# Attention kernel: keys transposed in rows of eight, first load and last store in pieces, plain copies as 32-bit words

## The chip, the cores and the metric

One core of a Trainium2 chip. The metric is the device time of one execution in microseconds (us). The kernel before takes 1265.33 us, the median of three runs (1265.04 to 1265.5).

## The reference

Softmax attention over 16 x 32 = 512 heads, bf16 in and out: 192 queries, 1024 keys, head size 128.

```python
B, H, Sq, Sk, D = 16, 32, 192, 1024, 128      # q, k, v: normal * 0.05, bf16
scale = q.shape[-1] ** -0.5
scores = jnp.einsum("bhqd,bhkd->bhqk", q, k) * scale
p = softmax(scores, axis=-1)
return jnp.einsum("bhqk,bhkd->bhqd", p, v)
```

## The kernel before

**Units.** The 512 heads come in 32 groups of 16 (G). A group is eight pairs of heads, and a pair is three units of 128 query rows: rows 0 to 127 of head a, the same of head b, and the last 64 rows of a and b together (two matmuls side by side on column halves of the array, `tile_position`). So there are 768 units, 24 to a group; three units are called a triple here.

**A unit's way.** `qk` (L199): two matmuls of 512 keys each, queries stationary, keys `kt` moving, into a score tile `s_ps` (two buffers). `rowmax` (L296, VectorE): one pass that scales, copies the scores to `ss` and takes the row's extreme into `nb`. Then x = scores minus extreme: for units 0 and 1 of a triple GpSimd subtracts (`shift`, L184) and the exp comes later; for unit 2 ScalarE does the exp at once (`exp_first`, L349 on, instruction L356). `tr` (L236): eight 128x128 transposes of x by TensorE into `pt_ps`; each loads a block of x as the weights and multiplies by `ident`. `evac` (L362, ScalarE): from `pt_ps` to `pt_sb`, with the exp for units 0 and 1 (L367) and as a plain copy for unit 2 (L369). `pv` (L247): eight products of `pt_sb` blocks with `vs`, each with a product by `ones` for the row sum (L270) where ScalarE has not summed already. `onorm` (L313, VectorE): division, into `ob`.

**Which keys stand in which block.** `vs` holds key 8p+t on partition p in block t, because its load reads eight keys of a row group as one contiguous run. `kt` holds the keys in their order, so block t of the transposes is every eighth column of x (`X[:, t: SK: KT_TILES]`, L244).

**Order.** Each engine has its own program, tied by semaphores. TensorE's is written out by hand (L286 to L292): at step s it issues `qk(s+1)`, `tr(s-4)`, `pv(s-7)`.

**Transfers.** SP alone issues them, all on one queue, in this order for each group g: `loads(g+2)` = the transposing DMA of 16 heads of k (L141, 4 MB, after the last `qk` of group g), that of q (L144), the plain load of v (L149, after the last `pv` of g); then `stores(g)` = three DMAs (L158, L163, L164, after the last `onorm` of g). `kt`, `qt`, `vs` and `ob` have two buffers. At the start the loads of groups 0 and 1 are issued without a wait. `qk` of a group's first unit waits for that group's k and q (L203, L204), `pv` of it for v (L251).

Of the kernel before, what the change touches and what calls it, by code (L numbers as in the profile page):

```python
# [5 lines left out]
BF16 = mybir.dt.bfloat16  # L6
F32 = mybir.dt.float32
# [5 lines left out]
R_W = 2  # L13


def _attention_kernel(nc, q, k, v, out, G=16, NS=2, LAGS=(2, 4, 5, 7), ROUTES=(R_W, R_W, R_EA)):
    B, H, SQ, D = q.shape
    SK = k.shape[2]
    assert D == 128 and SK == 1024 and SQ == 192, (D, SK, SQ)
# [43 lines left out]
    with ExitStack() as es:  # L63
# [6 lines left out]
        def sem(name):  # L70
            return es.enter_context(nc.semaphore(name))

        kt = sb("kt", [128, NS, G * SK], BF16)
        qt = sb("qt", [128, NS, G * SQ], BF16)
        vs = sb("vs", [128, NS, G, KT_TILES, 128], BF16)
        ob = sb("ob", [128, NSO, PPG, 4, 128], BF16)
# [5 lines left out]
        rinv = sb("rinv", [128, 2, 4], F32)  # L82
        ones = sb("ones", [128, 128], BF16)
        ident = sb("ident", [128, 128], BF16)
        s_ps = [ps("s_ps%d" % i, [128, SK], F32) for i in range(2)]
        pt_ps = [ps("pt_ps%d" % i, [128, KT_TILES, 128], BF16) for i in range(2)]
        o_ps = [ps("o_ps%d" % i, [128, 4, 128], F32) for i in range(2)]
        s_setup = sem("s_setup")
        sxk = [sem("sxk%d" % i) for i in range(NS)]
        sxq = [sem("sxq%d" % i) for i in range(NS)]  # L90
        svl = [sem("svl%d" % i) for i in range(NS)]
        sst = [sem("sst%d" % i) for i in range(NSO)]
        s_qk = sem("s_qk")
        s_max = sem("s_max")
# [17 lines left out]

        O_SLOT = (0, 2, 1)

        def load_cnt(g):
            return 16 * (g // NS + 1)

        def store_cnt(g):
            return 48 * (g // NSO + 1)
# [12 lines left out]

        @block.sync
        def _(e):
            def loads(g):
                s = g % NS
                last_u = (g - NS + 1) * UPG - 1
                h0 = g * G
                if g >= NS:
                    e.wait_ge(s_qk, last_u + 1)  # L140
                e.dma_start_transpose(  # L141
                    kt[:, s], kf[h0:h0 + G].rearrange("g k d -> (g k) d")
                ).then_inc(sxk[s], 16)
                e.dma_start_transpose(  # L144
                    qt[:, s], qf[h0:h0 + G].rearrange("g k d -> (g k) d")
                ).then_inc(sxq[s], 16)
                if g >= NS:
                    e.wait_ge(s_pv, last_u + 1)
                e.dma_start(  # L149
                    vs[:, s], vf[h0:h0 + G].rearrange("g (p t) d -> p g t d", t=KT_TILES)  # L150
                ).then_inc(svl[s], 16)

            def stores(g):
                so = g % NSO
                e.wait_ge(s_on, (g + 1) * PPG)
                h0 = g * G
                og = of[h0:h0 + G]
                e.dma_start(  # L158
                    og[:, 0:128, :].rearrange("h p d -> p h d"),
                    ob[:, so].rearrange("p pg (x y) d -> p (pg x) (y d)", y=2)[:, :, 0:128],  # L160
                ).then_inc(sst[so], 16)
                oab = og[:, 128:192, :].rearrange("(pg x) p d -> x p pg d", x=2)
                e.dma_start(oab[0], ob[0:64, so, :, 1, :]).then_inc(sst[so], 16)  # L163
                e.dma_start(oab[1], ob[64:128, so, :, 1, :]).then_inc(sst[so], 16)  # L164

            for g in range(min(NS, NGR)):
                loads(g)
            for g in range(NGR):
                if g + NS < NGR:
                    loads(g + NS)  # L170
                stores(g)
            for so in range(min(NSO, NGR)):
                n_uses = len(range(so, NGR, NSO))
                e.wait_ge(sst[so], 48 * n_uses)

        @block.gpsimd
# [21 lines left out]
        def _(pe):  # L198
            def qk(u):  # L199
                pr, k3, g, pg = unit_info(u)  # L200
                s = g % NS
                if u % UPG == 0:
                    pe.wait_ge(sxk[s], load_cnt(g))  # L203
                    pe.wait_ge(sxq[s], load_cnt(g))  # L204
                if u >= 2:
                    pe.wait_ge(s_max, u - 1)
                S = s_ps[u % 2]
                a = 2 * pg
                b = 2 * pg + 1
                ins = None  # L210
                for c in range(2):
                    cs = slice(512 * c, 512 * c + 512)
                    if k3 < 2:
                        x = a if k3 == 0 else b
                        ins = pe.matmul(  # L215
                            S[:, cs],
                            qt[:, s, x * SQ: x * SQ + 128],
                            kt[:, s, x * SK + 512 * c: x * SK + 512 * c + 512],
                            start=True, stop=True,
                        )  # L220
                    else:
                        pe.matmul(  # L222
                            S[0:64, cs],
                            qt[:, s, a * SQ + 128: a * SQ + 192],
                            kt[:, s, a * SK + 512 * c: a * SK + 512 * c + 512],
                            start=True, stop=True, tile_position=(0, 0),
                        )
                        ins = pe.matmul(  # L228
                            S[64:128, cs],
                            qt[:, s, b * SQ + 128: b * SQ + 192],  # L230
                            kt[:, s, b * SK + 512 * c: b * SK + 512 * c + 512],
                            start=True, stop=True, tile_position=(0, 64),
                        )
                ins.then_inc(s_qk, 1)

            def tr(u):  # L236
                wait_x(pe, u)
                if u >= 2:
                    wait_evac(pe, u - 2)
                X = x_sb[:, u % NX, :]  # L240
                PT = pt_ps[u % 2]
                ins = None
                for t in range(KT_TILES):
                    ins = pe.transpose(PT[:, t, :], X[:, t: SK: KT_TILES], ident[:])  # L244
                ins.then_inc(s_tr, 1)

            def pv(u):  # L247
                pr, k3, g, pg = unit_info(u)
                s = g % NS
                if u % UPG == 0:  # L250
                    pe.wait_ge(svl[s], load_cnt(g))  # L251
                wait_evac(pe, u)
                if k3 == 0 and pr >= 2:
                    pe.wait_ge(s_on, pr - 1)
                O = o_ps[pr % 2]
                PTS = pt_sb[:, u % NPT]
                sl = O_SLOT[k3]
                a = 2 * pg
                b = 2 * pg + 1
                ins = None  # L260
                with_rs = route(u) == R_W
                for t in range(KT_TILES):
                    first = t == 0
                    last = t == KT_TILES - 1
                    if k3 < 2:
                        x = a if k3 == 0 else b
                        ins = pe.matmul(O[:, sl, :], PTS[:, t, :], vs[:, s, x, t, :],  # L267
                                        start=first, stop=last, skip_group_check=True)
                        if with_rs:
                            ins = pe.matmul(O[:, 3, sl: sl + 1], PTS[:, t, :], ones[:, 0:1],  # L270
                                            start=False, stop=last, skip_group_check=True)
                    else:
                        pe.matmul(O[0:64, sl, :], PTS[:, t, 0:64], vs[:, s, a, t, :],  # L273
                                  start=first, stop=last, skip_group_check=True, tile_position=(0, 0))
                        ins = pe.matmul(O[64:128, sl, :], PTS[:, t, 64:128], vs[:, s, b, t, :],  # L275
                                        start=first, stop=last, skip_group_check=True, tile_position=(0, 64))
                        if with_rs:
                            pe.matmul(O[0:64, 3, sl: sl + 1], PTS[:, t, 0:64], ones[:, 0:1],
                                      start=False, stop=last, skip_group_check=True, tile_position=(0, 0))
                            ins = pe.matmul(O[64:128, 3, sl: sl + 1], PTS[:, t, 64:128], ones[:, 0:1],  # L280
                                            start=False, stop=last, skip_group_check=True, tile_position=(0, 64))
                ins.then_inc(s_pv, 1)
# [12 lines left out]
        def _(dve):  # L295
            def rowmax(u):  # L296
                dve.wait_ge(s_qk, u + 1)
                if u >= NSS:
                    wait_x(dve, u - NSS)
                dve.tensor_scalar(  # L300
                    ss[:, u % NSS, :], s_ps[u % 2][:], -scale, None, ALU.mult, ALU.min,
                    accum_out=nb[:, u % NSS: u % NSS + 1],
                ).then_inc(s_max, 1)

# [43 lines left out]
        def _(act):  # L348
# [13 lines left out]
            def evac(u):  # L362
# [3 lines left out]
                if route(u) == R_W:  # L366
                    act.activation(pt_sb[:, u % NPT], pt_ps[u % 2][:], ACT_FN.Exp, scale=-1.0).then_inc(s_eva, 1)  # L367
                else:
                    act.activation(pt_sb[:, u % NPT], pt_ps[u % 2][:], ACT_FN.Copy).then_inc(s_eva, 1)  # L369

            for step in range(NU + L_EV + 1):
                u = step - L_EV
# [43 lines left out]
```

## Time and profile before

| | us |
|---|---|
| median of three runs | 1265.33 |
| span of the profiled execution, first to last instruction | 1263.1 |
| so around the span | 2.2 |
| TensorE busy (matmuls / weight loads) | 1234.2 / 1009.4 |
| VectorE / ScalarE / GpSimd busy | 1102.0 / 1048.6 / 960.4 |
| bytes moved | 321.89 MB, 255 GB/s over the span |
| first matmul / first `pv` | 21.0 / 33.2 |
| last `pv` matmul issued / last instruction | 1256.6 / 1263.1 |

A group line of the profile reads: source line, engine, operation, output <- inputs, shapes, count, then total busy time and the mean ns of one; behind the bar the idle time of the engine just before. PE is TensorE's matmul side and PEld its weight loads. In the timeline and the chain of waits the first column is the start and the second the duration, both in us. SPq is SyncE's queue: the duration of a DMA there is the time in which it is issued, not that in which it lands.

### The profile page before, as it was taken

The page shows a single profiled execution, that of the slowest core. Times are in us where ns is not written, and L with a number is a line of the kernel's source. Part 1 is how long each engine was busy: PE and PEld are TensorE (multiplying, and loading weights), DVE is VectorE, ACT ScalarE, POOL GpSimd, SP SyncE. Part 2 cuts the span into 40 slices and gives each one's busy share as a digit, 9 for nine tenths or more (in the row PEclk, how much of TensorE's full clock was granted, in tenths as well). Part 3 has the DMA queues.
Part 4 walks back from the last instruction along what each step waited for, and adds up shares of the span by engine and source line. Part 5 has one row for each costly group of instructions (what it writes and reads, how often), then busy time and mean ns, then how long its engine had stood idle before and what let it go on. Part 6 is the DMA issues. An engine that isn't in the chain of part 4 may idle for free.

```text
span 1263.1 us, 48658 instructions
## 1 busy us (share of the span) xinstructions
PE 1234.2 (98%) x20480; PEld 1009.4 (80%) x20480; DVE 1102.0 (87%) x2304; ACT 1048.6 (83%) x1281; POOL 960.4 (76%) x518
## 2 busy tenths in 40 slices
PE   3999999999999999999999999999999999999997
PEld 1888888888888888888888888888888888888886
DVE  2889888898988989898898988889898898989885
ACT  1888888888888888888888888888888888888886
POOL 2778777777877778787777877777787777878774
PEclk9999999999999999999999999999999999999999
DMA  9999999999999999999999999999999999999941
GB/s 288 268 261 240 278 280 266 288 270 245 254 269 261 279 233 255 281 275 262 261 230 272 271 276 268 252 251 272 272 267 281 253 263 252 271 261 281 244 118 27
DMA packets 790743, 321.89 MB, mean 255 GB/s; under 512 B 724992, under 2 KB 724992, under 8 KB 790528
## 3 DMA queue, kind: packets, MB, share of 16 engines
q1 hardware_dynamic: 790528, 318.78, 108.8%
q8 instruction: 164, 2.69, 0.8%
q14 instruction: 51, 0.42, 0.1%
HBM read 134.22 MB, written 25.17 MB: 126 GB/s over the span
## 4 chain that ended last, share of the span: by engine, by line
PE 97%; SPq 1%; DMA 1%; ACT 0%; issue 0%; DVE 0%; ACTq 0%
PE pt_ps L244 33%; PE o_ps L267 24%; PE s_ps L215 18%; PE o_ps L273 11%; PE s_ps L222 9%; SPq L141 1%; DMA vs<-in_v_dram 1%; PE o_ps L270 1%; PE o_ps L275 1%; SPq L144 0%; PE s_ps L228 0%; ACT x_sb L356 0%; ACT pt_sb L367 0%; DVE ob L330 0%; DVE rinv L327 0%
## 5 line engine op out<-in xcount | busy, mean ns | idle before, releaser
L188 POOL TENSOR_TENSOR x_sb<-ss,nb 128x1024 bf16<-128x1024 f32 x512 | 959.7, 1895 | 288.9 <-PE pt_ps L244 266.8
L300 DVE TENSOR_SCALAR_CACHE_REDUCE ss<-s_ps 128x1024 f32<-128x1024 f32 x768 | 938.5, 1222 | 140.5 <-PE s_ps L215 110.8
L244 PEld LDWEIGHTS pt_ps<-ident,x_sb 128*128 128x128 bf16 x6144 | 487.1, 148 | 203.3 <-issue 105.4
L367 ACT ACTIVATE pt_sb<-pt_ps 128x1024 bf16<-128x1024 bf16 x512 | 521.0, 1018 | 41.9 <-PE pt_ps L244 41.8
L244 PE MATMUL pt_ps<-ident,x_sb 128*128 128x128 bf16 x6144 | 520.7, 228 | 0.2 <-ACT pt_sb L367 0.2
L267 PE MATMUL o_ps<-vs,pt_sb 128*128 128x128 bf16 x4096 | 403.0, 217 | 0.3 <-DMA vs<-in_v_dram 0.3
L369 ACT ACTIVATE pt_sb<-pt_ps 128x1024 bf16<-128x1024 bf16 x256 | 262.1, 1024 | 140.1 <-PE pt_ps L244 140.0
L270 PE MATMUL o_ps<-ones,pt_sb 128*128 128x1 bf16 x4096 | 376.0, 165 | 0.0
L267 PEld LDWEIGHTS o_ps<-vs,pt_sb 128*128 128x128 bf16 x4096 | 352.3, 97 | 0.5 <-DMA vs<-in_v_dram 0.4
L270 PEld LDWEIGHTS o_ps<-ones,pt_sb 128*128 128x128 bf16 x4096 | 340.7, 96 | 0.0
L215 PE MATMUL s_ps<-kt,qt 128*128 128x512 bf16 x1024 | 305.3, 379 | 21.3 <-DMA qt<-in_q_dram 21.0
L356 ACT ACTIVATE x_sb<-ss,nb 128x1024 bf16<-128x1024 f32 x256 | 292.3, 1142 | 23.6 <-DVE ss L300 23.6
L273 PE MATMUL o_ps<-vs,pt_sb 128*64 128x128 bf16 x2048 | 162.3, 222 | 0.0
L275 PE MATMUL o_ps<-vs,pt_sb 128*64 128x128 bf16 x2048 | 162.3, 222 | 0.0
L222 PE MATMUL s_ps<-kt,qt 128*64 128x512 bf16 x512 | 153.2, 381 | 0.6 <-DVE ss L300 0.5
L228 PE MATMUL s_ps<-kt,qt 128*64 128x512 bf16 x512 | 153.2, 381 | 0.0
L330 DVE TENSOR_TENSOR ob<-o_ps,rinv 128x384 bf16<-128x384 f32 x256 | 142.7, 557 | 8.7
L273 PEld LDWEIGHTS o_ps<-vs,pt_sb 128*64 128x64 bf16 x2048 | 121.0, 109 | 17.1
L275 PEld LDWEIGHTS o_ps<-vs,pt_sb 128*64 128x64 bf16 x2048 | 121.0, 109 | 0.0
L215 PEld LDWEIGHTS s_ps<-kt,qt 128*128 128x128 bf16 x1024 | 63.3, 96 | 23.6 <-issue 21.5
L300 DVE DVE_READ_ACCUMULATOR ss<-s_ps 128x1 f32 x768 | 64.0, 83 | 0.0
L356 ACT ACTIVATION_READ_ACCUMULATOR x_sb<-ss,nb 128x1 f32 x256 | 48.9, 191 | 0.0
(11 smaller groups left out, 165.7 us busy)
## 6 DMA issues: line engine op xcount, KB each, us to landing
vs<-in_v_dram SPq DMA_DIRECT2D x32, 4096.0 KB, 15.2
out_dram<-ob SPq DMA_DIRECT2D x32, 512.0 KB, 15.9
out_dram<-ob SPq DMA_DIRECT2D x64, 128.0 KB, 4.9
kt<-in_k_dram SPq DMA_TRANSPOSE x32, 21.4
qt<-in_q_dram SPq DMA_TRANSPOSE x32, 6.6
```

The source lines that it names most:

```text
L188: gp.tensor_tensor(x_sb[:, u % NX, :], ss[:, u % NSS, :], nb[:, u % NSS: u % NSS + 1].to_broadcast([128, SK]), ALU.subtract,).then_inc(s_x ...
L215: ins = pe.matmul(S[:, cs], qt[:, s, x * SQ: x * SQ + 128], kt[:, s, x * SK + 512 * c: x * SK + 512 * c + 512], start=True, stop=True,)
L222: pe.matmul(S[0:64, cs], qt[:, s, a * SQ + 128: a * SQ + 192], kt[:, s, a * SK + 512 * c: a * SK + 512 * c + 512], start=True, stop=True, ...
L244: ins = pe.transpose(PT[:, t, :], X[:, t: SK: KT_TILES], ident[:])
L267: ins = pe.matmul(O[:, sl, :], PTS[:, t, :], vs[:, s, x, t, :], start=first, stop=last, skip_group_check=True)
L270: ins = pe.matmul(O[:, 3, sl: sl + 1], PTS[:, t, :], ones[:, 0:1], start=False, stop=last, skip_group_check=True)
L273: pe.matmul(O[0:64, sl, :], PTS[:, t, 0:64], vs[:, s, a, t, :], start=first, stop=last, skip_group_check=True, tile_position=(0, 0))
L275: ins = pe.matmul(O[64:128, sl, :], PTS[:, t, 64:128], vs[:, s, b, t, :], start=first, stop=last, skip_group_check=True, tile_position=(0, ...
L300: dve.tensor_scalar(ss[:, u % NSS, :], s_ps[u % 2][:], -scale, None, ALU.mult, ALU.min, accum_out=nb[:, u % NSS: u % NSS + 1],).then_inc(s ...
L356: act.activation(x_sb[:, u % NX, :], ss[:, u % NSS, :], ACT_FN.Exp, bias=nb[:, u % NSS: u % NSS + 1], scale=-1.0, accum_out=rs[:, pr % NRS ...
L367: act.activation(pt_sb[:, u % NPT], pt_ps[u % 2][:], ACT_FN.Exp, scale=-1.0).then_inc(s_eva, 1)
L369: act.activation(pt_sb[:, u % NPT], pt_ps[u % 2][:], ACT_FN.Copy).then_inc(s_eva, 1)
```

## The change

1. **k** is read as rows of eight keys: a group's k is seen as 2048 rows of 1024 elements, and the transposing DMA writes `kt` as [128, 8, 2048]: block t holds key 8p+t of every head. A `qk` matmul now reads four runs of 128 columns, 4 KB apart, in place of one run of 512; the scores come out in the order of blocks, so that the transposes take packed runs of 128 columns.
2. **First group** loaded in three pieces (heads 0-1, 2-7, 8-15), each with semaphores of its own, in the order k0 q0, k1 q1 v0 v1, k2 q2 v2. **Last group** stored in four pieces (pairs 0-3, 4-5, 6, 7), three DMAs each.
3. **Plain copies** of unit 2 (L369) treat two bf16 numbers as one 32-bit word.

```diff
-def _attention_kernel(..., ROUTES=(R_W, R_W, R_EA)):
+def _attention_kernel(..., ROUTES=(R_W, R_W, R_EA),
+                      FIRST=((0, 2), (2, 8), (8, 16)), LAST=((0, 4), (4, 6), (6, 7), (7, 8))):
...
-        kt = sb("kt", [128, NS, G * SK], BF16)
+        kt = sb("kt", [128, NS, KT_TILES, G * 128], BF16)
...
+        def words(t):
+            return t.rearrange("p t q -> p (t q)").bitcast(F32)
...
+            def load_kq(g, a, b, sems):
+                s = g % NS
+                h0 = g * G
+                e.dma_start_transpose(
+                    kt[:, s, :, a * 128:b * 128],
+                    kf[h0 + a:h0 + b].rearrange("g (p t) d -> (g p) (t d)", t=KT_TILES),
+                ).then_inc(sems[0], 16)
+                e.dma_start_transpose(
+                    qt[:, s, a * SQ:b * SQ],
+                    qf[h0 + a:h0 + b].rearrange("g r d -> (g r) d"),
+                ).then_inc(sems[1], 16)
...
-            for g in range(min(NS, NGR)):
+            n = len(FIRST)
+            for i in range(n):
+                load_kq(0, *FIRST[i], (sf[i], sf[i]))
+                if i > 0:
+                    for i2 in range(i if i > 1 else 0, i + 1):
+                        load_v(0, *FIRST[i2], sfv[i2])
+            for g in range(1, min(NS, NGR)):
                 loads(g)
             for g in range(NGR):
                 if g + NS < NGR:
                     loads(g + NS)
-                stores(g)
+                for a, b in (LAST if g == NGR - 1 else ((0, PPG),)):
+                    stores(g, a, b)
...
-                if u % UPG == 0:
+                if g == 0:
+                    for i, (h, _) in enumerate(FIRST):
+                        if u == 3 * h // 2:
+                            pe.wait_ge(sf[i], 32)
+                elif u % UPG == 0:
                     pe.wait_ge(sxk[s], load_cnt(g))
                     pe.wait_ge(sxq[s], load_cnt(g))
...
-                    ins = pe.transpose(PT[:, t, :], X[:, t: SK: KT_TILES], ident[:])
+                    ins = pe.transpose(PT[:, t, :], X[:, t * 128:t * 128 + 128], ident[:])
...
-                    act.activation(pt_sb[:, u % NPT], pt_ps[u % 2][:], ACT_FN.Copy).then_inc(s_eva, 1)
+                    act.activation(words(pt_sb[:, u % NPT]), words(pt_ps[u % 2][:]), ACT_FN.Copy).then_inc(s_eva, 1)
```

Not shown: the same split of `loads` and `stores` into pieces a to b, `pv`'s waits for the pieces of v (`sfv`), and the counts of the semaphores.

More of the change, by code (lines that the diff above doesn't have):

```diff
@@ L13, with _attention_kernel @@
 R_W = 2
-def _attention_kernel(nc, q, k, v, out, G=16, NS=2, LAGS=(2, 4, 5, 7), ROUTES=(R_W, R_W, R_EA)):
+def _attention_kernel(nc, q, k, v, out, G=16, NS=2, LAGS=(2, 4, 5, 7), ROUTES=(R_W, R_W, R_EA),
+                      FIRST=((0, 2), (2, 8), (8, 16)), LAST=((0, 4), (4, 6), (6, 7), (7, 8))):
     B, H, SQ, D = q.shape
@@ L84, in _attention_kernel @@
         ident = sb("ident", [128, 128], BF16)
-        s_ps = [ps("s_ps%d" % i, [128, SK], F32) for i in range(2)]
+        s_ps = [ps("s_ps%d" % i, [128, KT_TILES, 128], F32) for i in range(2)]
         pt_ps = [ps("pt_ps%d" % i, [128, KT_TILES, 128], BF16) for i in range(2)]
@@ L91, in _attention_kernel @@
         svl = [sem("svl%d" % i) for i in range(NS)]
+        sf = [sem("sf%d" % i) for i in range(len(FIRST))]
+        sfv = [sem("sfv%d" % i) for i in range(len(FIRST))]
         sst = [sem("sst%d" % i) for i in range(NSO)]
@@ L113, in _attention_kernel @@
         O_SLOT = (0, 2, 1)
+        def words(t):
+            return t.rearrange("p t q -> p (t q)").bitcast(F32)
         def load_cnt(g):
-            return 16 * (g // NS + 1)
+            return 16 * (g // NS + 1 - (g % NS == 0))
         def store_cnt(g):
@@ L134, in _, with load_v @@
         def _(e):
+            def load_kq(g, a, b, sems):
[9 more added lines that the diff above has]
+                ).then_inc(sems[1], 16)
+            def load_v(g, a, b, sm):
+                h0 = g * G
+                e.dma_start(
+                    vs[:, g % NS, a:b],
+                    vf[h0 + a:h0 + b].rearrange("g (p t) d -> p g t d", t=KT_TILES),
+                ).then_inc(sm, 16)
             def loads(g):
@@ L137, in loads, with stores @@
                 last_u = (g - NS + 1) * UPG - 1
-                h0 = g * G
                 if g >= NS:
                     e.wait_ge(s_qk, last_u + 1)
[L141 to L146, printed above, removed]
+                load_kq(g, 0, G, (sxk[s], sxq[s]))
                 if g >= NS:
                     e.wait_ge(s_pv, last_u + 1)
[L149 to L153, printed above, removed]
+                load_v(g, 0, G, svl[s])
+            def stores(g, a, b):
                 so = g % NSO
-                e.wait_ge(s_on, (g + 1) * PPG)
-                h0 = g * G
-                og = of[h0:h0 + G]
+                e.wait_ge(s_on, g * PPG + b)
+                og = of[g * G + 2 * a:g * G + 2 * b]
                 e.dma_start(
                     og[:, 0:128, :].rearrange("h p d -> p h d"),
-                    ob[:, so].rearrange("p pg (x y) d -> p (pg x) (y d)", y=2)[:, :, 0:128],
+                    ob[:, so, a:b].rearrange("p pg (x y) d -> p (pg x) (y d)", y=2)[:, :, 0:128],
                 ).then_inc(sst[so], 16)
                 oab = og[:, 128:192, :].rearrange("(pg x) p d -> x p pg d", x=2)
-                e.dma_start(oab[0], ob[0:64, so, :, 1, :]).then_inc(sst[so], 16)
-                e.dma_start(oab[1], ob[64:128, so, :, 1, :]).then_inc(sst[so], 16)
-            for g in range(min(NS, NGR)):
+                e.dma_start(oab[0], ob[0:64, so, a:b, 1, :]).then_inc(sst[so], 16)
+                e.dma_start(oab[1], ob[64:128, so, a:b, 1, :]).then_inc(sst[so], 16)
+            n = len(FIRST)
[5 more added lines that the diff above has]
+            for g in range(1, min(NS, NGR)):
                 loads(g)
@@ L170, in _ @@
                     loads(g + NS)
-                stores(g)
+                for a, b in (LAST if g == NGR - 1 else ((0, PPG),)):
+                    stores(g, a, b)
             for so in range(min(NSO, NGR)):
                 n_uses = len(range(so, NGR, NSO))
+                if so == (NGR - 1) % NSO:
+                    n_uses += len(LAST) - 1
                 e.wait_ge(sst[so], 48 * n_uses)
@@ L201, in qk @@
                 s = g % NS
-                if u % UPG == 0:
+                a = 2 * pg
+                b = 2 * pg + 1
+                if g == 0:
[3 more added lines that the diff above has]
+                elif u % UPG == 0:
                     pe.wait_ge(sxk[s], load_cnt(g))
@@ L207, in qk, with keys @@
                 S = s_ps[u % 2]
-                a = 2 * pg
-                b = 2 * pg + 1
                 ins = None
                 for c in range(2):
-                    cs = slice(512 * c, 512 * c + 512)
+                    cs = slice(4 * c, 4 * c + 4)
+                    def keys(x):
+                        return kt[:, s, cs, x * 128:x * 128 + 128]
                     if k3 < 2:
@@ L216, in qk @@
                             S[:, cs],
-                            qt[:, s, x * SQ: x * SQ + 128],
-                            kt[:, s, x * SK + 512 * c: x * SK + 512 * c + 512],
+                            qt[:, s, x * SQ:x * SQ + 128],
+                            keys(x),
                             start=True, stop=True,
@@ L223, in qk @@
                             S[0:64, cs],
-                            qt[:, s, a * SQ + 128: a * SQ + 192],
-                            kt[:, s, a * SK + 512 * c: a * SK + 512 * c + 512],
+                            qt[:, s, a * SQ + 128:a * SQ + 192],
+                            keys(a),
                             start=True, stop=True, tile_position=(0, 0),
@@ L229, in qk @@
                             S[64:128, cs],
-                            qt[:, s, b * SQ + 128: b * SQ + 192],
-                            kt[:, s, b * SK + 512 * c: b * SK + 512 * c + 512],
+                            qt[:, s, b * SQ + 128:b * SQ + 192],
+                            keys(b),
                             start=True, stop=True, tile_position=(0, 64),
@@ L249, in pv @@
                 s = g % NS
-                if u % UPG == 0:
+                if g == 0:
+                    for i, (h, _) in enumerate(FIRST):
+                        if u == 3 * h // 2:
+                            pe.wait_ge(sfv[i], 16)
+                elif u % UPG == 0:
                     pe.wait_ge(svl[s], load_cnt(g))
@@ L300, in rowmax @@
                 dve.tensor_scalar(
-                    ss[:, u % NSS, :], s_ps[u % 2][:], -scale, None, ALU.mult, ALU.min,
+                    ss[:, u % NSS, :], s_ps[u % 2][:].rearrange("p t k -> p (t k)"), -scale, None, ALU.mult, ALU.min,
                     accum_out=nb[:, u % NSS: u % NSS + 1],
```

## The prediction

> **What bounds the kernel now.** I read the page's chain of waits first: it is TensorE for 97%, so the steady state is TensorE's own stream. Then the groups, for the price of one instruction.
>
> ```profile
> PE 97%; SPq 1%; DMA 1%; ACT 0%; issue 0%; DVE 0%; ACTq 0%
> ...
> L244 PEld LDWEIGHTS pt_ps<-ident,x_sb 128*128 128x128 bf16 x6144 | 487.1, 148 | 203.3 <-issue 105.4
> ...
> L267 PEld LDWEIGHTS o_ps<-vs,pt_sb 128*128 128x128 bf16 x4096 | 352.3, 97 | 0.5 <-DMA vs<-in_v_dram 0.4
> ```
>
> The reader is to see two weight loads of the same shape: the one that takes every eighth column (L244) lasts 148 ns, the packed one (L267) 97.
>
> Third, the chain in order of time, in one triple around 600 us. It repeats exactly every 4.80 us (a group, eight triples: 38.4 us; 256 triples: 1229 us).
>
> ```profile
> 602.40 0.50 PE pt_ps L244 x8
> 602.90 0.17 PE o_ps L273
> 603.07 0.00 PE o_ps L275
> 603.08 0.05 PE o_ps L273
> ...
> 603.90 0.65 PE pt_ps L244 x8
> 604.55 0.06 PE o_ps L267
> ```
>
> Eight transposes take 0.50, 0.50 and 0.65 us in the three units; the packed products L273, with as many columns, follow each other at 0.055 us.
>
> The fourth view decides: SP's timeline, one group.
>
> ```profile
> 595.90 19.96 SPq L141 DMA_TRANSPOSE kt<-in_k_dram  x1
> 615.91 3.94 SPq L144 DMA_TRANSPOSE qt<-in_q_dram  x1
> 619.89 0.59 SPq L149 DMA_DIRECT2D vs<-in_v_dram  x1
> 620.52 5.06 SPq L158 DMA_DIRECT2D out_dram<-ob  x1
> 625.63 9.81 SPq L163 DMA_DIRECT2D out_dram<-ob  x1
> 635.48 1.59 SPq L164 DMA_DIRECT2D out_dram<-ob  x1
> 637.11 17.95 SPq L141 DMA_TRANSPOSE kt<-in_k_dram  x1
> ```
>
> No time lies between one DMA and the next: SP is held back by the transfers, not by TensorE. From group 3's L141 (101.85 us) to group 26's (978.34) the queue is never free, and a turn takes 876.5 / 23 = **38.1 us**. TensorE needs 38.4. So the transfers are a second bound 0.3 us per group below the first, and whatever TensorE gains beyond that must be waited for. Only at the end do packets pause for TensorE: three gaps of 0.3, 2.0 and 1.8 us from 1054 on. The view by windows shows the rates (last three columns: clock, DMA share, GB/s):
>
> ```profile
> 6.00:16.00 10.00, 0.00 (x0) 0.00 (x0) 0.00 (x0) 0.00 (x0) 0.00 (x0) 1.00 1.28 290
> 25.00:30.00 5.00, 4.68 (x22) 1.90 (x21) 4.38 (x9) 2.25 (x3) 4.87 (x4) 1.00 1.04 392
> 690.00:691.00 1.00, 1.00 (x17) 0.77 (x14) 0.97 (x6) 1.00 (x2) 1.00 (x1) 1.00 1.95 22
> 1258.50:1260.00 1.50, 0.00 (x0) 0.00 (x0) 0.00 (x0) 0.00 (x0) 0.00 (x0) 0.88 0.97 221
> ```
>
> k alone, in 256 B packets: 290 GB/s, so 4.19 MB cost 14.5 us. v, in 2 KB packets: 392. The stores' 256 B pieces: 221. And some five times a group, beside a 16 KB instruction fetch (164 such packets on the page's queue 8), a transpose falls to 22 GB/s for about 1.2 us. These stalls are part of the 38.1.
>
> **The change, part by part.**
>
> *Transposes (0.19 us per triple).* A packed pitch of 0.0556 us gives 8 x 0.0556 = 0.445 for 0.494, a gain of 0.049; in the unit before L273, where the last gap of 0.155 stays, 0.045. In the unit that follows the half-width products, the first weight load starts only when these have drained, and the first two transposes are 113 ns apart; packed, after a stall, L267 to L270 at 33.2 us are 66: 0.047 more, 0.097 in all. Together 0.191 x 256 = 48.9 us of TensorE; the triple takes 4.61 us, the group **36.9**. The others have room: VectorE is busy 34.4 of 38.4 us per group, ScalarE 32.7, GpSimd 30.0.
>
> The Trainium skill ("TensorE: Matmul & The Clock Gate", section "Weight-path perf modes") says that fast weight load takes its columns "packed or strided", with which this part would gain nothing. The 148 against 97 ns speak against it.
>
> *qk reads four runs.* No row has such a read. From below 0, since the same 512 columns stream and the pitch of 0.213 us is already that of the columns; from above, the pitch of single 128-column products against a quarter of a 512 one (55.6 against 213.5 / 4 = 53.4 ns) gives 9 ns per product, six a triple, 0.05 us, 14 us in all. I take 0; the next paragraph hides either.
>
> *k's DMA: the unknown.* The same 4 MB, but neighbouring rows of a tile are now 2 KB apart, and a row is 2 KB long. If it is read in 2 KB packets, at v's 392 GB/s, it takes 10.7 us, 3.8 less. If the pitch costs what the stores' scattered 256 B pieces pay (221), 19.0, 4.5 more. I take 0: the nearest row is L141 itself, with as many 256 B blocks to the same tiles.
>
> The skill ("DMA: Bandwidth & Descriptors", section "Latency and other measured facts") has a DMA transpose at 261 GB/s where a middle dimension is not contiguous and 350 to 400 where all is. The 290 lies between; 261 would add 1.6 us per group and end near 1295, 350 would take 2.5 off and leave TensorE the bound.
>
> *First group in pieces.* qk starts after 1/8 of k and q: at 290 GB/s 2.1 us of data instead of 17, so near 6 us for 21.0; the second piece lands near 12, so unit 3 comes some 12 us sooner than at 24.5. But group 1's q lands at 48.1 + 6.6 (median) = 54.7, and is used at 57.8: only 3.1 us of that can be kept. The queue is full from 2 us on and moves the same bytes; two more turns between transposes and v, at about 1 us (rates dip so at 20 and 54 us), make everything behind **2** us later.
>
> *Last group in pieces.* From the last L158 (1257.46) to the end 5.6 us pass: 786 KB at 221 GB/s (3.6) and 2 to land. The last piece is an eighth: three issues (0.4 to 0.65 each) and the landing, some 3.4. Gain **2.2** (0 to 3.5).
>
> *Word copies.* 256 copies of 1.02 us for 1024 elements get down to half at best; that they get longer is excluded, since L356 reads 1024 32-bit elements in 1.14 and these read 512. ScalarE has 0.7 us idle per triple, and `pv` comes three steps (4.8 us) after the copy. 0; without that cover up to 0.5 us a triple. The waits for pieces stand in TensorE's stream, where `tr` and `pv` queue behind; priced above.
>
> **Sum.** When does each group's q land, when does TensorE come? Before: q of group 31 at 1188.0 + 6.6 = 1194.6, used at 1209.8 (v: 1207.2 for 1223.6). After: landing 1194.6 + 2 - 4.1 (the gaps close) = 1192.5. TensorE alone, from group 1 at 56.7 with 36.9 per group: 1163.7. So it waits from about group 6 on, and the landing sets the end. From group 31's first qk to the end it was 1263.1 - 1209.8 = 53.3; 29 units of transposes at 0.064 take off 1.9, the store 2.2: 49.2. Span 1192.5 + 49.2 = 1241.7, time with the 2.2 around it **1244 us** (-1.7%). Of 48.9 us of faster TensorE some three quarters become a wait.
>
> **Rivals.** *A, the forecast: transfers set the pace, k as dear as now.* A turn varied: groups 4 to 9 took 37.2, 10 to 19 38.5. Over 28 groups that is -26 to +10: 1218 to 1254, and I allow to 1268 for where the fetches fall.
> *B, k in long packets, TensorE bound.* A turn is 34.3. q of group 1 lands at 54.7 + 2 - 7.6 = 49; 30 x 36.9 later 1156, + 49.2 + 2.2 = 1207. For it: rows are now 2 KB and contiguous. Against: each block of a tile is still 128 columns.
> *C, k dearer: slower.* With 0.7 us more per group ((1265.3 - 1244) / 32; 277 GB/s) the whole gain is gone. Halfway to the stores' rate, 255 GB/s, k takes 16.4: 32 x 1.9 = 61, so 1305; at 221 it is 1388. For it: the margin is 5% of one DMA, and 256 B pieces at a pitch are the slowest row. Against: those are writes.
> *D, the packed load changes nothing at the pitch:* TensorE stays at 38.4, group 1's 3.1 - 2 and the store's 2.2 remain: 1262.
>
> **How the numbers follow.** About 0.2% (2.5 us) is what a measurement can tell from no change. A 0.52 (faster 0.47, same 0.02, slower 0.03), B 0.18, C 0.25, D 0.05 (0.03 faster, 0.02 same). Faster 0.68, same 0.04, slower 0.28. 1200 to 1300 leaves out the upper half of C and a little of B, some 0.16.
>
> **What the profile after would show.** L244's weight load near 97 ns and its eight in 0.445; qk or pv idle before the group's first unit, released by a DMA, for some 1.2 us per group; L141 issued in about 18 us, the rate at 290 in undisturbed stretches, packets still 724,000 under 512 B. If the packets fall to about a third of that, it is B; if the rate in quiet stretches is under 277, C. If TensorE is at 97% of the chain with a triple of 4.61, the second bound was misread.

## The result, and the profile after

The changed kernel takes 1260.79 us (median of five runs, 1252.79 to 1263.23) beside 1265.33 us before (1264.81 to 1265.58): ratio 0.9948, interval 0.9931 to 0.9965. A second set of runs gave 1253.56 (1249.98 to 1258.57), ratio 0.9909 (0.9892 to 0.9927). So it is faster, by 0.5 to 0.9%, where 1.7% was forecast; and a kernel whose runs lay within 0.8 us of each other has become one whose runs spread over 9 to 10. The profiled execution took 1261.43 us (span 1259.7).

From the page after: share of the chain, packets, the transposes' weight load, the plain copy.

```profile
DMA packets 791048, 321.90 MB, mean 256 GB/s; under 512 B 725296, under 2 KB 725296, under 8 KB 790832
...
PE 91%; DMA 4%; SPq 3%; issue 3%; DVE 0%
...
L277 PEld LDWEIGHTS pt_ps<-ident,x_sb 128*128 128x128 bf16 x6144 | 388.2, 98 | 229.9 <-issue 110.6
...
L406 ACT ACTIVATE pt_sb<-pt_ps 128x512 f32<-128x512 f32 x256 | 152.9, 597 | 133.0 <-PE pt_ps L277 132.9
```

The weight load is down from 148 to 98 ns, the copy from 1.02 to 0.60 us, and k still comes in 725,000 packets under 512 B. TensorE has 91% of the chain in place of 97; the rest went to transfers. The chain in order of time (start, duration, what) shows the three kinds of transposes:

```profile
599.66 0.45 PE pt_ps L277 x8
600.10 0.17 PE o_ps L310
...
601.10 0.55 PE pt_ps L277 x8
...
602.74 0.45 PE pt_ps L277 x8
```

0.45, 0.55 and 0.45 for 0.50, 0.65 and 0.50 in the chain before. A triple in which nothing waits takes 4.61 us for 4.80, so a group 36.85 for 38.4; over all triples, those at a lower clock among them, the transposes lost 0.18 us on average. But TensorE waits. Its waits over the span (total, times, longest; the first product alone accounts for the 6.3):

```profile
PE s_ps L248 <- issue: 38.8, 22, 8.6
PE s_ps L248 <- DMA qt<-in_q_dram: 16.1, 3, 6.3
```

L248 is `qk` of a group's first unit, which starts some 6 us after q's issue, when q lands; where no releaser is named ("issue"), it is the same wait. The faster transposes save 256 x 0.18 = 46 us and TensorE starts 14.6 us sooner; 48.6 us of that (38.8 + 16.1 - 6.3) is this wait alone. SP's timeline shows why: the start, then the first and the last k of the steady state.

```profile
0.80 1.44 SPq L144 DMA_TRANSPOSE kt<-in_k_dram  x1
2.30 1.51 SPq L148 DMA_TRANSPOSE qt<-in_q_dram  x1
3.85 6.73 SPq L144 DMA_TRANSPOSE kt<-in_k_dram  x1
...
29.20 0.58 SPq L155 DMA_DIRECT2D vs<-in_v_dram  x1
29.83 26.05 SPq L144 DMA_TRANSPOSE kt<-in_k_dram  x1
...
59.67 0.58 SPq L155 DMA_DIRECT2D vs<-in_v_dram  x1
...
110.70 18.02 SPq L144 DMA_TRANSPOSE kt<-in_k_dram  x1
...
1186.35 17.91 SPq L144 DMA_TRANSPOSE kt<-in_k_dram  x1
1204.31 3.97 SPq L148 DMA_TRANSPOSE qt<-in_q_dram  x1
```

Group 3's k is issued at 110.70, **8.85** us later than before (101.85), not 2. From there 28 turns take 1075.65 us, **38.42** each, not 38.0. These two terms make the whole miss of this execution: 6.85 + 28 x 0.42 = 18.6 us, and q of the last group is issued at 1204.3 where the sum had it at 1185.9. What follows was as forecast: from that group's first `qk` (1210.4) to the end 49.3 us, for 49.2.

### The profile page after: what moved, and what is told of

It is laid out like the page before. It is cut to its first block, busy times and chain, and to the rows that moved or that the text cites. A ratio compares the mean times of both kernels' runs of the same rounds, so it can differ in the third digit from the quotient of the medians.

```text
span 1259.7 us, 48676 instructions
## 1 busy us (share of the span) xinstructions
PE 1197.8 (95%) x20480; PEld 934.2 (74%) x20480; DVE 1096.6 (87%) x2304; ACT 938.9 (75%) x1281; POOL 960.2 (76%) x518
## 4 chain that ended last, share of the span: by engine, by line
PE 91%; DMA 4%; SPq 3%; issue 3%; DVE 0%
PE pt_ps L277 28%; PE o_ps L304 24%; PE s_ps L248 18%; PE o_ps L310 11%; PE s_ps L255 8%; DMA kt<-in_k_dram 2%; SPq L144 2%; DMA vs<-in_v_dram 1%; PE o_ps L307 1%; SPq L148 1%; PE o_ps L312 1%; PE s_ps L261 0%; SPq L155 0%; DVE ob L367 0%; DVE rinv L364 0%
## 5 line engine op out<-in xcount | busy, mean ns | idle before, releaser
L404 ACT ACTIVATE pt_sb<-pt_ps 128x1024 bf16<-128x1024 bf16 x512 | 521.1, 1018 | 171.3 <-PE pt_ps L277 171.3
L277 PEld LDWEIGHTS pt_ps<-ident,x_sb 128*128 128x128 bf16 x6144 | 388.2, 98 | 229.9 <-issue 110.6
L277 PE MATMUL pt_ps<-ident,x_sb 128*128 128x128 bf16 x6144 | 474.3, 220 | 0.0
L248 PE MATMUL s_ps<-kt,qt 128*128 128x512 bf16 x1024 | 308.4, 383 | 54.8 <-issue 38.8
L406 ACT ACTIVATE pt_sb<-pt_ps 128x512 f32<-128x512 f32 x256 | 152.9, 597 | 133.0 <-PE pt_ps L277 132.9
L248 PEld LDWEIGHTS s_ps<-kt,qt 128*128 128x128 bf16 x1024 | 63.8, 97 | 58.9 <-issue 48.2
L364 DVE RECIPROCAL rinv<-o_ps 128x2 f32<-128x2 f32 x256 | 42.6, 166 | 8.3 <-PE o_ps L312 7.5
```

The lines of the kernel that those rows point to most:

```text
L248: ins = pe.matmul(S[:, cs], qt[:, s, x * SQ:x * SQ + 128], keys(x), start=True, stop=True,)
L277: ins = pe.transpose(PT[:, t, :], X[:, t * 128:t * 128 + 128], ident[:])
```

## The experiments

All times in us. "v1" and "k3" are the moments in the profiled execution at which SP issues group 1's v and group 3's k; "turn" is the mean distance of the k DMAs from group 3 to 31; "stalled" is the time per turn, counted in the trace's packet records, in which the transposing DMAs run below 30% of their full rate while v is not running either. These columns belong to the profiled execution, which can lie anywhere in the range: for the changed kernel it took 1261.4 and 1258.6 us (the longest of its second set), for the first group whole 1240.5 and 1246.5, so turns of two kernels differ by more here than their medians do.

| kernel | median (range) | ratio to before (interval) | v1 | k3 | turn | stalled |
|---|---|---|---|---|---|---|
| before | 1265.3 | | 52.3 | 101.9 | 38.16 | 5.43 |
| changed | 1260.8 (1252.8–1263.2) | 0.9948 (0.9931–0.9965) | 59.7 | 110.7 | 38.42 | 5.80 |
| changed, again | 1253.6 (1250.0–1258.6) | 0.9909 (0.9892–0.9927) | 56.8 | 108.6 | 38.40 | 5.75 |
| first group whole | 1244.6 (1240.2–1253.2) | 0.9844 (0.9818–0.9869) | 53.1 | 104.1 | 37.92 | 5.29 |
| first group whole, again | 1246.1 (1242.6–1248.1) | 0.9847 (0.9835–0.9860) | 53.3 | 105.5 | 38.11 | 5.53 |
| layout alone | 1244.1 (1241.6–1248.5) | 0.9839 (0.9824–0.9854) | 51.2 | 101.3 | 38.07 | 5.51 |
| copies as bf16 | 1254.0 (1252.6–1258.8) | 0.9920 (0.9907–0.9932) | 58.6 | 109.6 | 38.34 | 5.73 |
| k in rows of one key | 1254.2 (1251.1–1258.9) | 0.9916 (0.9900–0.9931) | 56.9 | 108.3 | 38.42 | 5.80 |
| pieces and words alone | 1265.3 (1263.8–1266.6) | 1.0004 (0.9995–1.0012) | 56.1 | 108.3 | 38.00 | 5.48 |
| v twice | 1218.5 (1216.6–1220.5) | 0.9635 (0.9621–0.9649) | 57.6 | 97.7 | 36.85 | |
| one row sum | 1244.0 (1241.1–1247.6) | 0.9828 (0.9815–0.9840) | 57.5 | 109.5 | 38.00 | 5.66 |
| v on ScalarE's queue | 1302.8 (1298.4–1311.9) | 1.0310 (1.0278–1.0342) | 56.8 | 107.7 | 39.60 | |
| the same, first group whole | 1300.6 (1295.5–1304.2) | 1.0278 (1.0260–1.0297) | 53.1 | 104.0 | 39.56 | |
| pieces, TensorE held | 1251.8 (1249.0–1254.3) | 0.9894 (0.9880–0.9908) | 55.8 | 105.8 | 38.20 | 5.60 |
| pieces, v last | 1253.1 (1248.9–1257.3) | 0.9904 (0.9884–0.9924) | 58.0 | 109.5 | 38.31 | 5.70 |
| stores on ScalarE's queue | 1222.2 (1219.9–1237.6) | 0.9679 (0.9643–0.9714) | 54.0 | 93.1 | 37.08 | |
| the same, again | 1222.1 (1219.3–1225.0) | 0.9662 (0.9649–0.9675) | 53.3 | 92.8 | 37.08 | |
| the same, first group in pieces | 1226.0 (1224.8–1226.5) | 0.9689 (0.9677–0.9702) | 58.8 | 99.1 | 37.08 | |

(v1 of the two kernels with v on ScalarE's queue is group 1's, which SP still issues.)

### The parts of the change

**The first group whole.**

```diff
-                      FIRST=((0, 2), (2, 8), (8, 16)), ...
+                      FIRST=((0, 16),), ...
```

(In the loop of the first loads v then follows q at once.)

> The changed kernel with the first group loaded whole again (k, q, v of 16 heads, one DMA each); all else as changed. Theory 1 (one transfer queue sets the pace, and the pieces put extra turns between transposes and plain loads into it): group 3's k is issued near 102 us instead of 110.7, everything behind is 7 to 9 us earlier, the time falls from 1260.8 to about 1253. Theory 2 (k's DMA in rows of eight keys is itself dearer, which also makes the start late): group 3's k still near 110, time 1259 to 1262. If the early start of TensorE were worth what it was built for, the time would rise by some 10 us.

SP's timeline of the profiled execution:

```profile
15.73 3.18 SPq L148 DMA_TRANSPOSE qt<-in_q_dram  x1
18.96 0.59 SPq L155 DMA_DIRECT2D vs<-in_v_dram  x1
...
53.08 0.58 SPq L155 DMA_DIRECT2D vs<-in_v_dram  x1
...
104.13 17.72 SPq L144 DMA_TRANSPOSE kt<-in_k_dram  x1
```

TensorE begins at 21.1 in place of 6.3, and the kernel is *faster* than the changed one, by 16.2 us against its first set and 9.0 against its second: group 3's k goes out 6.6 us sooner than in the changed kernel's first profile, and the turn is shorter as well. Beside others on one chip it came again:

> The first group loaded whole again, beside the other three on one chip. The changed kernel itself gave 1260.8 and 1253.6 us in two sets, so this one is expected at 1240 to 1248 us, as it was (1244.6), with group 3's k issued near 104 us and a turn of 37.9 to 38.2 us.

**k's rows undone, transposes packed.** k is read as before and `kt` is plain, so that scores and v stand in different orders of keys.

```diff
-                    kt[:, s, :, a * 128:b * 128],
-                    kf[h0 + a:h0 + b].rearrange("g (p t) d -> (g p) (t d)", t=KT_TILES),
+                    kt[:, s, a * SK:b * SK],
+                    kf[h0 + a:h0 + b].rearrange("g k d -> (g k) d"),
```

> The changed kernel with k transposed in rows of one key as before (256 B rows, one run of 512 per qk), and packed blocks for the transposes all the same; keys and values are then matched wrongly, the amount of work is the same. Theory 1 (the block pitch costs nothing): turn of the queue 38.4 as in the changed kernel, time within 3 us of 1260.8. Theory 2 (rows 2 KB apart make k's DMA dearer by some 0.3 us per group): turn 38.1, time about 1250.

The same turn as the changed kernel, 38.42, and its second set's time: the new rows cost k nothing and bring nothing.

**Old layout, strided transposes; pieces and words alone** (the edit above, and `X[:, t: SK: KT_TILES]` again).

> The kernel before with the pieces at both ends and the 32-bit copies alone: k in rows of one key, transposes of every eighth column. Theory 1: TensorE 38.4 us per group again, queue 38.1 to 38.4, about equal; start late by 7 to 9 us as in the changed kernel, end earlier by 2: 1264 to 1272, so slower than before or equal, and only 0 to 10 us above the changed kernel, though its transposes cost 48 us more of TensorE. A theory without the second bound has it 47 us above the changed kernel.

Ratio 1.0004: without the packing TensorE takes 38.4 us per group again (weight load 148 ns), and a TensorE that starts at 5.6 instead of 21.0 gains nothing. Group 3's k is as late as in the changed kernel, 108.3.

**The layout alone**: first group whole, last group stored whole, copies as bf16.

> k's new rows with the packed transposes alone: first group whole, last group stored whole, copies as bf16. My theory: 2.2 us above the kernel that differs from it in the last group's store and the copies (1244.6 us before, so about 1247 us), that is 18 us faster than the kernel before (ratio 0.986). Rival (the store in pieces gains nothing or costs): the same as that kernel or faster, 1240 to 1245 us.

1244.1, all of the gain. The store in pieces does what it should in the trace: from the last `pv` matmul to the end 6.8 us here and before, 4.3 to 5.2 in every profile with the pieces. But in the medians, with runs 7 us apart, these 2 us can't be seen; that expectation was too fine for the measurement.

**The copies as bf16 again**, the rest as changed.

> The changed kernel with its plain copies as 1024 bf16 elements again, 1.02 us in place of 0.60. My theory (ScalarE is not on the path, the copies are used three steps later): within 3 us of the changed kernel, 1253 to 1262 us, turn 38.4 us. Rival (ScalarE's time per unit decides when a pt buffer is free, now that TensorE's triple is 4.61 us): slower by up to 0.4 us a triple, up to 100 us.

No difference from the changed kernel: the 0.43 us per copy lie beside other work.

### Is it the transfers?

**v loaded only for groups 0 and 1**; later groups use these.

> The changed kernel with v loaded only for groups 0 and 1; the later groups multiply by the values that lie in the buffer, so 30 of 32 loads of v are left out. Theory 1: a turn of the queue falls by about 11 us to 27, TensorE is the bound alone, at 36.9 to 37.0 us per group; from the first qk of group 1 (near 62 us) 30 x 36.95 + 49, so 1215 to 1222. A theory in which TensorE itself lost what the packed loads gave (qk with four runs dearer, another engine late): no change, 1255 to 1262.

With 126 MB less to move, TensorE runs at 36.85 us per group without a wait from group 2 on, and the gain that was hidden comes out. So the packing is worth what was forecast, and the queue hides it.

**Fewer instructions to fetch.** The row sum's product with `ones` only for the last block, 7168 TensorE instructions fewer (the divisor is then an eighth of the true one).

> The changed kernel with the product by the ones column (row sum) issued for the last of eight blocks only, so that 7168 of 40960 TensorE instructions, and with them about one instruction fetch of 16 KB in six, are left out (the divisor is then one eighth of the sum). TensorE is not the bound, so that alone gives nothing. Theory 'instruction fetches stall the transposes and are part of a turn': 0.9 fetches fewer per group, most of them in transposes at 1.2 us each, a turn 0.7 to 1.0 us shorter, time 1230 to 1240. Rival, 'a turn is data alone': turn 38.4, time 1256 to 1262.

136 fetches of 16 KB in place of 164, 38.00 for 38.40 us per turn, 9.6 us less than the changed kernel on the same chip: the direction is that of the fetches, the size about half of what was expected. The packet records show why: of 0.9 fetches fewer per turn only 0.34 lay in k and q (2.66 in place of 3.00); the others lay beside v and the stores. 0.34 x 1.2 us makes 0.4 us, what the turn lost.

**v from ScalarE's queue**, for groups 2 on.

```diff
+                    if u >= UPG and u % UPG == NPT - 1 and u // UPG + 1 < NGR:
+                        act.wait_ge(s_pv, u - NPT + 1)
+                        g = u // UPG + 1
+                        act.dma_start(vs[:, g % NS], vf[g * G:g * G + G]...).then_inc(svl[g % NS], 16)
```

> The changed kernel with v of groups 2 to 31 issued from ScalarE, on its own queue, right after the evacuation whose wait already says that the buffer is free; k, q and the stores stay on SP's. Theory 1, in the form 'one queue in order sets the pace: while a transpose stands still for an instruction fetch, or one DMA drains before the next, nothing else moves': v fills those times, a turn falls below TensorE's 36.9, and the time goes to 1218 to 1225 as with v loaded twice only. Rival, 'the 16 engines' total work is the bound': v costs the transposes what it gains, 1250 to 1262.

The page's queues, and one us by windows (last three columns: clock, DMA share, GB/s):

```profile
q1 hardware_dynamic: 728912, 192.95, 78.6%
q10 hardware_dynamic: 61920, 125.83, 33.4%
```

```profile
642.00:643.00 1.00, 1.00 (x22) 0.59 (x17) 0.97 (x5) 1.00 (x2) 1.00 (x1) 1.00 0.15 46
```

Slower by 3.1%, and my first theory in the form "only the order on one queue counts" fell. Where both queues have work, the packet records show 43 GB/s of 256 B packets beside 345 GB/s of 2 KB ones: 0.168 packets per ns of each, one for one, so that the transpose falls to a seventh of its rate. And an instruction fetch, beside which v alone keeps some 365 GB/s in the packet records of the kernel before, now stalls both (46 GB/s at 642). The Trainium skill ("DMA: Bandwidth & Descriptors", section "Queues, rings and completion order") says that each DMA engine goes round the queues that have work; the equal numbers of packets agree with that. The same with the first group whole gave the same loss:

> The first group whole and v on ScalarE's queue: the version that theory 1 points to. TensorE bound from group 1 on: its first qk near 56 in place of 61.7, then 30 x 36.95 and 51 to the end: 1213 to 1218. If the engines' total work is the bound: 1240 to 1247, as with the first group whole alone.

**The stores from ScalarE's queue**, first group whole. One of a group's three stores behind `exp_first` of each of three successive triples, where what it waits for is done; the last group's stay on SP.

```diff
+                    n = u // 3 - NRS + 1
+                    if n >= PPG and n % PPG < 3 and n // PPG < NGR:
+                        stores(act, n // PPG - 1, 0, PPG, (n % PPG,))
```

> First group whole, and the stores of groups 0 to 30 are issued from ScalarE's queue, one DMA in each of three successive triples; the last group's stores stay where they were. Theory 1 (the turn is the sum of the transfers' times and the tails between one kind and the next; the store phase takes some 5 us for 2.7 us of data and could lie beside the next transpose): a turn of 36.5 to 37 us, TensorE becomes the bound at 36.9 us per group, 1212 to 1225 us. Rival (as with v on that queue: two queues alternate packet for packet, the transpose is prolonged by what the other queue gains, and a fetch holds both up): a turn of 38 us or more, 1244 us or slower, with L142's k issue longer than 18 us beside the stores.

SP's timeline, one group, and TensorE's waits over the whole span:

```profile
577.03 25.40 SPq L159 DMA_TRANSPOSE kt<-in_k_dram  x1
602.47 5.82 SPq L163 DMA_TRANSPOSE qt<-in_q_dram  x1
608.33 0.58 SPq L170 DMA_DIRECT2D vs<-in_v_dram  x1
613.88 25.09 SPq L159 DMA_TRANSPOSE kt<-in_k_dram  x1
```

```profile
PE s_ps L249 <- DMA qt<-in_q_dram: 21.4, 1, 21.4
PE s_ps L249 <- issue: 3.7, 4, 1.4
```

k's issue is longer, 25 us for 18, as the rival said; but the three stores no longer stand in the queue (14 to 15 us of issue time per turn), and SP is idle for 5 us before each k (608.91 to 613.88): it waits for TensorE. TensorE waits at the start, and 3.7 us in all after it. The bounds have changed places, and 1222 us is the best time of all kernels here that load every v, 3.2 to 3.4% below before.

### What the pieces of the first group cost

With pieces, group 1's v is issued at 56 to 60 us, with the group whole at 51 to 54. Group 3's k, where SP issues everything and TensorE is not held, goes out at 109.2 on average in seven profiles with pieces (108.3 to 110.7) and at 103.2 in four with the group whole, the kernel before among them (101.3 to 105.5): **6.0** us. Two tests of what this is made of:

**TensorE held** until all three pieces of k and q are there (`if u == 0` in place of `if u == 3 * h // 2`).

> The first group in pieces as in the changed kernel, but TensorE's first product waits for all three pieces of k and q. The six profiles with a first group whole or in pieces have group 1's v issued at 51.2 to 53.3 us (whole) and 56.8 to 59.7 us (pieces). Theory 1 (the additional turns from one DMA to the next cost this): still 56 to 58.5 us, since only the fetch at 26 us, 1.4 us, goes with the early start. Rival (TensorE's early start brings fetches and other traffic into the first loads): back to 51 to 54 us. The time itself gets longer with either, since k of group 2 waits for group 0's last qk, which comes some 9 us later than with a group loaded whole: 1255 to 1270 us.

**v's pieces last**, behind all of k and q.

> The same three pieces, but all of k and q first and the pieces of v behind them, so that a transposing DMA does not follow a plain one in the middle of the first group. Theory 1 (each turn between transposing and plain DMAs costs 1 to 1.5 us, each turn from k to q about 1): group 1's v issued 2 to 3 us sooner than in the changed kernel, 55 to 57 us, group 3's k near 106.5 us, time 2 to 4 us below the changed kernel, 1250 to 1256 us. Rival (the pieces' own small packets or the fetches cost it): no change, 57 to 60 us and 109 us.

Held, v1 is 55.8, short of both forecasts. Ten profiles with pieces have 57.7 on average and seven with the group whole 52.9, so some 3 of the 4.8 us stay with the pieces. It is one profile against a spread of 1 to 2 us: this split is an estimate. The time was forecast too high: held back to 30 us, the kernel is no slower than when TensorE starts at 6. With v last, v1 and k3 are what they were (58.0 and 109.5).

The packet records show more closely where the 6.0 us arise (a joint is the place where one DMA on the queue follows another of a different kind):

| | last packet of group 0's k and q | first packet of group 1's k |
|---|---|---|
| first group whole (before, whole, whole again, layout alone) | 20.4 to 20.7 | 31.4 to 31.7, mean 31.6 |
| pieces, v last | 23.7 | 34.7 |
| pieces, TensorE held | (v stands between) | 35.6 |
| pieces (seven profiles, v last among them) | (v stands between) | 34.7 to 37.7, mean 35.9 |

So 4.3 of the 6.0 us are lost within the first group's own loads, and 4.0 of them also where TensorE stands still: they belong to the pieces. With v last, where only four more joints between k and q are new until the last q, these joints alone cost 3.1 us, about 0.8 each; v's place among the transposes adds about 1. Fetches are a small part: up to 50 us there are two or three with pieces, two with the group whole and one with TensorE held. The other 1.7 us come later; with TensorE held they do not (k3 is 105.8, 2.6 above the group whole). Which wait brings them is not shown.

Windows of the changed kernel show two of the places (last three columns as above; the queue has work all the time):

```profile
5.80:7.20 1.40, 0.85 (x3) 0.33 (x4) 0.00 (x0) 0.00 (x0) 0.00 (x0) 1.00 1.24 177
```

```profile
26.50:30.50 4.00, 0.32 (x8) 0.20 (x6) 0.84 (x2) 0.81 (x1) 2.03 (x2) 0.79 1.10 136
```

From one piece to the next 177 GB/s, and from k through q to v, with a fetch, 136; with the group whole there are 290 from 6 to 16 us (k) and 394 from 25 to 30 (v).

**Pieces where TensorE is the bound.** The kernel with its stores on ScalarE's queue, with the first group in pieces and, beside it, whole.

> The kernel with its stores on ScalarE's queue (TensorE-bound, 1222 us), with the first group in pieces again. Theory 1 (group 1's q lands 5 to 6 us later with pieces, so that TensorE stands still in front of group 1 and the earlier start is lost): first qk of group 1 near 62 us in place of 58, some 4 us slower, 1224 to 1228 us. Rival (where TensorE is the bound, its earlier start counts): up to 15 us faster, 1207 to 1218 us.

> The stores on ScalarE's queue with the first group whole, beside the same with pieces: 1219 to 1225 us again, with one run in six perhaps near 1237.

3.9 us slower, as the first theory had it: first `qk` of group 1 at 60.8 in place of 56.9. TensorE has 15 us more time for group 0 and spends them in front of group 1.

## Why the prediction was right and wrong

- **Transposes: right.** 0.19 us per undisturbed triple as forecast, weight load 98 ns, a group 36.85 for 36.9. Packed against strided decided it in a pair that differs in nothing else (k in rows of one key against pieces and words alone: 98 and 148 ns). The Trainium skill ("TensorE: Matmul & The Clock Gate", section "Weight-path perf modes") lists the read pattern of fast weight load as "packed or strided" and gives no price for the step; for a step of eight columns these runs show 148 ns against 98.
- **qk reads four runs: 0, right** as far as it can be seen: with v loaded twice, a group takes the 36.85 us that the transposes alone account for.
- **k's DMA: 0, right**, shown by its rows undone: same turn, same 290 GB/s, same number of packets. Rivals B (long packets) and C (dearer k) fell. So did both figures that the prediction weighed from the Trainium skill ("DMA: Bandwidth & Descriptors", section "Latency and other measured facts"), 261 GB/s and 350 to 400: k moves at 290 in either layout.
- **The second bound: right.** TensorE waits from group 1 on (from group 4, 4 and 8 in three profiles with the first group whole; about 6 was forecast), and v taken away brings the hidden gain out.
- **First group in pieces, the step that failed:** "make everything behind 2 us later" measured 8.85 in the profiled execution and 6.0 between the averages. I had charged two more turns between transposing and plain DMAs and left out the four more joints between k and q. Those left out are the larger part: 3.1 us in the kernel with v last, while v's place adds about 1, and 4.0 us of the first group's loss stay with TensorE held. What adds the last 1.7 us behind the first group stays open. Of TensorE's earlier start 3.1 us were said to be the most that can be kept; with the queue setting the pace none of it is. With the term at 0 in place of 2, the sum gives 1242; the kernel that loads the first group whole measured 1244.6 and 1246.1.
- **The turn, the second term that failed:** 38.42 in place of 38.0, over 28 turns 11.6 us in the profiled execution. That is the upper end: the second set's profile has 38.40 at 1258.6 us, and its median is 5 us lower, so by an estimate that puts these 5 us on 28 turns, 38.2. The mean of a before in which TensorE set the pace was taken for a constant. In eleven of the twelve kernels with a figure in the table's last column, turn minus stalled time is 32.5 to 32.7 us (one row sum: 32.3): what varies is the stalls. About three per turn lie at a 16 KB fetch and last some 1.2 us. (The prediction had a transpose stalled five times a group; five fetches fall into a turn, but about two of them beside v and the stores.) Why the turn is longer with the first group in pieces is not settled. Pieces by themselves do not do it, as 38.00 in pieces and words alone (38.16 before) suggests, and the number of fetches that begin in k or q differs too little to tell (3.0 to 3.1 per turn with pieces and packed transposes, 3.0 whole, 2.8 before). Rival A's spread, 1218 to 1254, was for this, and the profiled run lies 7 us above it.
- **Last group in pieces: right** in the trace (4.3 to 5.2 for 6.8 us), not visible in medians. **Word copies: 0, right.**
- Rival D, 1262, is close to the first set's number and wrong in its mechanism: TensorE did get faster.

## What to carry to other kernels

Before a faster engine is priced, look for the next bound and its margin: here a queue that was never free stood 0.3 us per group behind TensorE, and of 49 us only 4 to 21 came out until the stores were taken off that queue. Where a queue is the bound, splitting its first transfers to start an engine sooner costs every joint (about 0.8 us each here) and gains nothing, because the engine catches up with the queue anyway. And a mean turn read while another engine sets the pace is no constant: give it the spread of the stalls inside it.

## What the runs showed of the hardware that was not expected

- Two queues with work share packet for packet. Beside 2 KB packets of v, the 256 B transposes get 43 GB/s for 290, and the kernel loses 49 us against the changed one on the same chip (1302.8 and 1253.6). Beside the stores, k's issue takes 25 us for 18, and the kernel gains 24 (1246.1 to 1222.2, on one chip). What is moved to the second queue decides.
- A 16 KB instruction fetch holds a transposing DMA up for some 1.2 us (22 GB/s for 290, at 690 us before), and a plain load too when both queues are at work (46 GB/s). Beside v alone, on one queue, the rate stays at some 365.
- With the transfers as the bound, runs of one kernel spread by 5 to 14 us; with TensorE as the bound by 1 to 6, except for one run of the kernel with stores on ScalarE's queue (1237.6 for 1222).
- The granted clock falls behind a wait: after the stretch at 26.5 to 30.5 us, in which TensorE was busy for 0.32 of 4 us (shown above), it was 0.59 in 34 to 36:

  ```profile
  34.00:36.00 2.00, 2.00 (x25) 1.46 (x23) 0.51 (x3) 1.02 (x1) 0.00 (x0) 0.59 1.05 309
  ```

  Over the span it is 0.986 for 0.999 before; in the kernel with stores on ScalarE's queue it is 0.999 again. That it costs nothing here, since the same groups then wait for q anyway, is argued and not tested.
